# Attention scores computed in quarters of the TensorE array for the first 8 and the last 7 groups

## The chip, the cores and the metric

The kernel runs on one core of one Trainium2 chip. The metric is the device time of one execution in microseconds (us), lower is better. PE is TensorE (matmuls), PEld its weight loads, DVE is VectorE, ACT is ScalarE, POOL is GpSimd, SP is SyncE, whose queue issues the DMAs.

## What is computed

```python
def reference(q, k, v, w_gate, w_val, w_out, w_in2, w_out2):
    # q, k, v: 4 batches x 8 heads x 576 positions x 64
    scores = np.where((rel >= 0) & (rel < 64), q @ k.T / 8, -1e9)   # rel = row - column
    x = softmax(scores) @ v                    # as 2304 tokens x 512
    g = x @ w_gate                             # 512 x 1536
    x = (g * sigmoid(g) * (x @ w_val)) @ w_out # 1536 x 512
    h = x @ w_in2                              # 512 x 2048
    return (h * np.clip(h + 3, 0, 6) / 6) @ w_out2
```

Inputs and outputs are float32; the weights arrive as 64-bit floats.

## The kernel before

**Attention** is cut into 36 groups: 9 stretches of 256 tokens by 4 pairs of heads, numbered `n = stretch * 4 + pair`. A group goes through five parts, each a function: `scores` (PE), `softmax_a` and `softmax_b` (DVE and ACT), `transposes` (PE), `evac_t` (a copy out of PSUM), `values` (PE) and `store_x` (a copy into the tokens `xr`, or through a tile `xg` to memory). A group holds four blocks of 64 queries (`GB = 4`). In `scores` the two heads of a pair share one matmul of the whole 128x128 array: the queries of head 0 stand in rows 0 to 63 and columns 0 to 63 of the stationary operand, those of head 1 in the other two 64s, and the rest of it is zeros, written by the host. So one group loads 128 partitions of 512 numbers of queries and 320 of keys (832 x 128 float32, 416 KB), and its scores are four matmuls into one PSUM bank. A float32 matmul stands in the trace as two matmul instructions. `values` uses halves of the array: an output of 64 rows for each head.

**Main part.** The first feed-forward layer takes the tokens in blocks of 512 (`t` = 0, 1, 2) and chunks `c` of 128 of the 1536 columns: 36 steps `n = 12 t + c`. A step's own matmuls are `gate` (12, into PSUM bank `g`), `val` (12, into `v`) and `ffn1_out` of the step before (12, into four `acc` banks), in a form with operands split into a high and a low part. The first 8 groups run before step 0 (`first_block`). The other 28 are threaded through the steps: `group_at` says which group's scores stand at the end of which step; its softmax and transposes come one step later, its values two. Before, groups 8 to 15 have steps 1 to 8, groups 16 to 25 steps 11 to 20, and groups 26 to 35 steps 22 to 31. Scores go to bank `c` and transposes to bank `d` at the end of a step, behind `ffn1_out`, and values to `d` between `gate` and `val`. Meanwhile `pump` runs the conversion of the 64-bit weights (tiles `raw`, `wf`, `wt`, `ws`) on ACT and DVE a few operations at a time.

**Order.** `first_block` and everything from step 24 on are in program order on every engine; steps 1 to 23 are ordered by the framework's scheduler.

**Later parts.** The last 768 tokens go through the first layer by a scheme with fewer products (`wide_chunk`). Then comes a loop over chunks `c` (`late_out`, the late outputs): each step of it has 12 matmuls with a moving operand of 384 columns, whose operand `uh`/`ul` was split one step ahead by `late_split` (a copy on ACT, a subtraction on DVE). Beside it `prep` makes the operands of the second feed-forward layer (`operands`: `upper` on ACT, `lower` and `minus` on DVE) in 11 pieces, two per step. The rest of the time is the second layer.

Of the kernel before, what the change touches and what calls it, by code (L numbers as in the profile page):

```python
# [19 lines left out]
B, H, S, D = 4, 8, 576, 64  # L20
WIN = 64
# [8 lines left out]
TB = 512  # L30
# [22 lines left out]
CONVERT_STOP = 12  # L53
LATER = -5
LATER_FROM = 26
FIRST_LOADS = (3, 5)
CONVERT_WIDE = (0, 0, 0, 1, 1, 1, 2)
SUMS_WIDE = (3, 1, 1, 1, 0, 0, 0)
X_STEPS = {7: 1, 8: 1, 9: 1, 10: 1, 11: 1}
SAVE_FROM = 6  # L60


# [4 lines left out]
@with_exitstack  # L67
def attention_two_ffn(ctx: ExitStack, tc, qk, v, w, out):
    nc = tc.nc
# [274 lines left out]
    def masks():  # L344
        nc.gpsimd.memset(mask, 0.0)
        for h in range(2):
            a = mask[64 * h:64 * h + 64, 0, :]
            nc.gpsimd.affine_select(
                out=a, in_=a, compare_op=ALU.is_ge, fill=MASKED / SCALE,
                base=-1, pattern=[[1, 128]], channel_multiplier=-1,  # L350
            )
            nc.gpsimd.affine_select(
                out=a, in_=a, compare_op=ALU.is_ge, fill=MASKED / SCALE,
                base=WIN, pattern=[[-1, 128]], channel_multiplier=1,
            )
        nc.gpsimd.memset(mask[:, 1, 0:64], MASKED / SCALE)
        nc.vector.tensor_copy(mask[:, 1, 64:128], mask[:, 0, 64:128])
        make_identity(nc, ident)
# [9 lines left out]
    def load_qk(n):  # L368
        t = a_tile("qk", [128, GB * 128 + WIN + GT])
        nc.sync.dma_start(out=t, in_=qk[n])  # L370
        a_held[n, "qk"] = t
# [6 lines left out]
    def scores(n, tag):  # L378
# [8 lines left out]
        a_held[n, "s"] = s  # L387

    def softmax_a(n):
        s = a_held.pop((n, "s"))  # L390
        y = a_tile("y", [128, GB, 128])
        nm = a_tile("s", [128, 3, GB])
        for u in range(GB):
            m = 1 if (n // NPAIR * GB + u) % (S // WIN) == 0 else 0
            nc.vector.tensor_tensor_reduce(  # L395
                out=y[:, u, :], in0=s[:, u * 128:(u + 1) * 128], in1=mask[:, m, :],
                scale=-SCALE, scalar=3.0e38, op0=ALU.add, op1=ALU.min,
                accum_out=nm[:, 0, u:u + 1],
            )
# [27 lines left out]
    def evac_t(n):  # L427
        t = a_held.pop((n, "t"))
        pt = a_tile("pt", [128, GB, 128])
        on_act = n % 2 or per_block <= n < 2 * per_block  # L430
        copy = nc.scalar.copy if on_act else nc.vector.tensor_copy
        copy(pt.rearrange("p a b -> p (a b)"), t)
        a_held[n, "pt"] = pt

    def values(n, tag, bufs=1):
        pt = a_held.pop((n, "pt"))
        vt = a_held.pop((n, "v"))
        o = psum(tag, bufs)
        for u in range(GB):
            for h in range(2):  # L440
                rows = slice(h * D, (h + 1) * D)
                nc.tensor.matmul(
                    o[rows, u * WIN:(u + 1) * WIN], vt[:, u, rows],
                    pt[:, u, h * WIN:(h + 1) * WIN], start=True, stop=True,
                )
        a_held[n, "o"] = o

    def store_x(n, xr):
        g, p = n // NPAIR, n % NPAIR
        o = a_held.pop((n, "o"))  # L450
        copy = nc.scalar.copy if n < 2 * per_block or n % 2 else nc.vector.tensor_copy
        if n < n_wide:
# [23 lines left out]
    def first_block():  # L476

        xr = new_x()
        with ExitStack() as st:
# [8 lines left out]
            for s in range(per_block + 6):  # L488
# [7 lines left out]
                at(softmax_b, s - 2)  # L496
                at(scores, s, "gc"[s % 2])
                at(transposes, s - 3, "vd"[s % 2])
# [471 lines left out]
    steps1 = [(t, c) for t in range(NB) for c in range(NC1)]  # L970
    group_at = {n: per_block + n - 1 for n in range(1, per_block + 1)}
    group_at.update({n + LATER + (n >= LATER_FROM): n for n in range(2 * per_block, n_groups)})

# [4 lines left out]
    with ExitStack() as fixed:  # L978
# [10 lines left out]
        for n, (t, c) in enumerate(steps1):  # L989
            if n == 0:  # L990
                start.enter_context(tc.manual_schedule())
            if n == 1:
                start.close()
# [11 lines left out]
            gate(t, c, both=last)  # L1005
            at(softmax_a, n - 1)
            pump(pumps // 2)
            at(softmax_b, n - 1)
# [4 lines left out]
            u = silu(t, c)  # L1013
            at(values, n - 2, "d" if t else "c")
            at(load_v, n - 1)
            at(store_x, n - 2, xr)
            val(t, c)
# [5 lines left out]
            if n:  # L1023
                ffn1_out(*steps1[n - 1])
            at(transposes, n - 1, "d")
            at(scores, n, "c")
            at(evac_t, n - 1)
# [60 lines left out]
        for c in range(NC1 - 1):  # L1088
            load_ring()
            late_split(c + 1)  # L1090
            late_out(c)
            advance(prep, 2)
        for _ in prep:
# [25 lines left out]
def _layout(q, k, v, w_gate, w_val, w_out, w_in2, w_out2):  # L1119
# [3 lines left out]
    def by_head(a):  # L1123

        return a.reshape(B, NPAIR, 2, S, D).transpose(1, 2, 0, 3, 4).reshape(NPAIR, 2, NT, D)

    qd = np.zeros((NG, NPAIR, 2, D, GB, 2, WIN), q.dtype)
    qr = by_head(q).reshape(NPAIR, 2, NG, GB, WIN, D).transpose(1, 2, 0, 5, 3, 4)
# [4 lines left out]
    kt = np.stack([kp[..., g * GT:g * GT + GT + WIN] for g in range(NG)])  # L1133
    qk = np.concatenate([qd.reshape(n, 128, GB * 128), kt.reshape(n, 128, GT + WIN)], axis=2)
    vp = np.zeros((B, NPAIR, 2, WIN + S, D), v.dtype)
    vp[:, :, :, WIN:] = v.reshape(B, NPAIR, 2, S, D)
# [11 lines left out]
    w = np.concatenate([w1.reshape(-1, 128, 512), w2.reshape(-1, 128, 512)])  # L1148
    return {"qk_t": c(qk), "v_t": vt, "w_t": c(w).view(np.int64)}

# [22 lines left out]
```

## Time and profile before

| | us |
|---|---|
| median of 3 runs (931.14 to 934.33) | 932.47 |
| the profiled execution | 935.44 |
| its span on the core | 933.7 |
| PE busy / DVE busy / ACT busy in the span | 901.0 / 703.3 / 418.1 |

The span reaches from the first to the last instruction; the 1.7 us that the execution's time has more lie around it. Times in the rows further down are us from the start of the span. Ends of matmuls are modelled, so what a piece of PE work costs is best read from the start of one row to the start of the next.

### The profile page before, as it was taken

What the parts mean: (1) busy time and instruction counts of PE and PEld (TensorE: products, weight loads), DVE (VectorE), ACT (ScalarE), POOL (GpSimd) and SP (SyncE); (2) the same over time, 40 slices, a digit from 0 to 9 for tenths busy, and PEclk for the clock granted to TensorE, in tenths of its full rate; (3) what the DMA queues carried; (4) which work ended last, traced back from release to release, by engine and by line L of the source; (5) the groups of instructions that cost most, each with busy time, mean ns of one, the idle gap of its engine ahead of it and who ended that gap; (6) DMA issues with size and microseconds to landing.
All of it is one profiled execution on the core that took longest, in us unless ns stands there. A gap on an engine that the chain in (4) does not pass through costs nothing.

```text
span 933.7 us, 14252 instructions
## 1 busy us (share of the span) xinstructions
PE 901.0 (97%) x4968; PEld 790.2 (85%) x4968; DVE 703.3 (75%) x1628; ACT 418.1 (45%) x995; POOL 2.2 (0%) x12
## 2 busy tenths in 40 slices
PE   5699999998999999999999999999999999999997
PEld 5587787887777888789999899898989898989896
DVE  6999999987987887788888647766666677565654
ACT  5778897656765755534444423121122121311111
POOL 0000000000000000000000000000000000000000
PEclk9799999999999999999999999999999999999999
DMA  8557997777885888507454487856568656485601
GB/s 328 168 166 215 359 336 280 266 244 254 265 314 182 305 315 273 191 6 241 148 175 141 169 327 278 297 196 210 180 244 306 217 191 216 152 321 190 216 23 68
DMA packets 67607, 209.47 MB, mean 224 GB/s; under 512 B 7248, under 2 KB 14416, under 8 KB 67152
## 3 DMA queue, kind: packets, MB, share of 16 engines
q1 hardware_dynamic: 67392, 208.43, 64.5%
q8 instruction: 39, 0.64, 0.3%
q14 instruction: 32, 0.26, 0.1%
q10 hardware_dynamic: 144, 0.13, 0.0%
HBM read 159.12 MB, written 49.41 MB: 223 GB/s over the span
## 4 chain that ended last, share of the span: by engine, by line
PE 69%; DVE 12%; DMA 11%; ACT 5%; issue 2%; SPq 0%; ACTq 0%; DVEq 0%
DMA raw<-w_t 7%; PE acc L859 5%; PE acc L860 5%; PE acc L858 5%; PE v L817 3%; PE v L819 3%; PE v L818 3%; PE g L817 3%; PE g L819 3%; PE g L818 3%; PE acc L561 3%; PE acc L562 3%; PE acc L560 3%; DMA w2d<-ws 2%; PE v L510 2%
## 5 line engine op out<-in xcount | busy, mean ns | idle before, releaser
L838 ACT CAST gh<-g 128x384 fp32r<-128x384 f32 x96 | 49.3, 514 | 195.9 <-DVE g L829 171.2
L840 DVE TENSOR_TENSOR gl<-g,gh 128x384 fp32r<-128x384 f32 x96 | 53.2, 555 | 45.3 <-ACT gh L838 43.9
L561 PE MATMUL acc<-ul,wt 128*128 128x512 f32 (+1 forms) x216 | 81.6, 378 | 0.5 <-DVE ul L538 0.5
L562 PE MATMUL acc<-uh,wt 128*128 128x512 f32 (+1 forms) x216 | 80.3, 372 | 0.0
L860 PE MATMUL acc<-wt,gl 128*128 128x512 f32 x192 | 75.2, 391 | 0.0
L859 PE MATMUL acc<-wt,gh 128*128 128x512 f32 x192 | 75.1, 391 | 0.0
L858 PE MATMUL acc<-wt,gh 128*128 128x512 f32 x192 | 74.7, 389 | 0.0
L560 PE MATMUL acc<-uh,wt 128*128 128x512 f32 (+1 forms) x216 | 73.4, 373 | 0.9 <-ACT uh L533 0.7
L510 PE MATMUL g<-xh,wt 128*128 128x512 f32 x144 | 60.2, 418 | 6.5 <-DVE u L546 4.1
L132 ACT ACTIVATE raw<-raw 128x512 int32<-128x512 uint32 x68 | 46.1, 679 | 42.1 <-DMA raw<-w_t 41.6
L401 ACT ACTIVATE y<-y,s 128x128 f32<-128x128 f32 x144 | 56.2, 394 | 14.6 <-DVE s L395 14.4
L510 PE MATMUL v<-xh,wt 128*128 128x512 f32 x144 | 58.4, 406 | 0.0
L511 PE MATMUL g<-xl,wt 128*128 128x512 f32 x144 | 57.8, 401 | 0.2 <-DVE xl L330 0.2
L512 PE MATMUL g<-xh,wt 128*128 128x512 f32 x144 | 57.5, 399 | 0.0
L817 PE MATMUL v<-xh,wt 128*128 128x384 f32 x168 | 56.8, 338 | 0.4 <-ACT q L904 0.4
L817 PE MATMUL g<-xh,wt 128*128 128x384 f32 x168 | 56.5, 337 | 0.0
L511 PE MATMUL v<-xl,wt 128*128 128x512 f32 x144 | 56.5, 393 | 0.0
L512 PE MATMUL v<-xh,wt 128*128 128x512 f32 x144 | 56.5, 392 | 0.0
L819 PE MATMUL v<-xh,wt 128*128 128x384 f32 x168 | 56.4, 336 | 0.0
L819 PE MATMUL g<-xh,wt 128*128 128x384 f32 x168 | 56.4, 336 | 0.0
L818 PE MATMUL v<-xl,wt 128*128 128x384 f32 x168 | 56.3, 335 | 0.0
L818 PE MATMUL g<-xl,wt 128*128 128x384 f32 x168 | 56.3, 335 | 0.0
(202 smaller groups left out, 2276.0 us busy)
## 6 DMA issues: line engine op xcount, KB each, us to landing
wt<-w2d SPq DMA_DIRECT2D x144, 512.0 KB, 4.8
raw<-w_t SPq DMA_DIRECT2D x68, 512.0 KB, 5.0
w2d<-ws SPq DMA_DIRECT2D x48, 512.0 KB, 4.7
wt<-w1d SPq DMA_DIRECT2D x33, 512.0 KB, 4.3
qk<-qk_t SPq DMA_DIRECT2D x36, 416.0 KB, 5.2
w1d<-wt SPq DMA_DIRECT2D x26, 512.0 KB, 5.4
v<-v_t SPq DMA_DIRECT2D x36, 256.0 KB, 4.9
x_out<-ob SPq DMA_DIRECT2D x17, 256.0 KB, 2.1
```

The lines of the kernel that those rows point to most:

```text
L510: nc.tensor.matmul(dst, wt[:, 0, col], hi, start=kc == 0, stop=False)
L511: nc.tensor.matmul(dst, wt[:, 0, col], lo, start=False, stop=False)
L512: nc.tensor.matmul(dst, wt[:, 1, col], hi, start=False, stop=kc == KC - 1)
L560: nc.tensor.matmul(a, wt[:, 0, col], hi, start=c == 0, stop=False)
L561: nc.tensor.matmul(a, wt[:, 0, col], lo, start=False, stop=False)
L562: nc.tensor.matmul(a, wt[:, 1, col], hi, start=False, stop=c == NC1 - 1)
L817: nc.tensor.matmul(dst, wt[:, 0, col], hi[:, k, :], start=k == 0, stop=False)
L818: nc.tensor.matmul(dst, wt[:, 0, col], lo[:, k, :], start=False, stop=False)
L819: nc.tensor.matmul(dst, wt[:, 1, col], hi[:, k, :], start=False, stop=k == 1)
L858: nc.tensor.matmul(a, hi[:, row], wt[:, 0, :], start=begin, stop=False)
L859: nc.tensor.matmul(a, hi[:, row], wt[:, 1, :], start=False, stop=False)
L860: nc.tensor.matmul(a, lo[:, row], wt[:, 0, :], start=False, stop=end)
```

## The change

Three things are done. **First**, groups 0 to 7 and 29 to 35 (`QUARTERS`) get their scores by `quarter_scores`: for each block of queries and each head one matmul with a stationary operand of 64 x 64 (no zeros) and 128 moving columns. The head sets the half of the array's rows, the parity of the block the half of its columns, so that four matmuls that follow each other lie in four quarters; head 0 writes to one PSUM bank and head 1 to another. Such a group loads 576 x 128 float32 (288 KB), from an input of its own. Softmax and values take the blocks in the new order; softmax has the same number of operations. **Second**, the groups stand at other steps: 8 to 15 at steps 1 to 8, group 24 at step 10, 16 to 23 at steps 11 to 18, 25 to 35 at steps 19, 20 and 22 to 30. From step 24 on, transposes (now in bank `v`), values (in the second half of bank `c`) and quarter scores (in the first halves of `c` and `d`) stand one behind the other at the end of the step, and `store_x` moves to the start of the next step but one; for groups 29 and up `evac_t` is always on ACT and `store_x` on DVE. **Third**, the loop of the late outputs makes one piece of `prep` per step in place of two. Around this, a part of the mask that belongs to the first block of a sequence is first written by GpSimd in two halves, since blocks now share a softmax operation's rows differently, and filled up at step 0.

```diff
-LATER = -5
-LATER_FROM = 26
...
+LAST_FROM, LAST_STEP = 29, 24
+EMPTY = (9, 21)
+QUARTERS = [*range(TB // GT * (H // 2)), *range(LAST_FROM, NG * (H // 2))]
+WHOLE = [n for n in range(NG * (H // 2)) if n not in QUARTERS]
...
-        nc.gpsimd.memset(mask[:, 1, 0:64], MASKED / SCALE)
+        nc.gpsimd.memset(mask[0:64, 1, 0:64], MASKED / SCALE)
+        nc.gpsimd.tensor_copy(mask[64:128, 1, 0:64], mask[64:128, 0, 0:64])
...
     def load_qk(n):
-        t = a_tile("qk", [128, GB * 128 + WIN + GT])
-        nc.sync.dma_start(out=t, in_=qk[n])
+        if n in QUARTERS:
+            t = a_tile("qk", [128, GT + WIN + GT])
+            nc.sync.dma_start(out=t, in_=qq[QUARTERS.index(n)])
+        else:
+            t = a_tile("qk", [128, GB * 128 + WIN + GT])
+            nc.sync.dma_start(out=t, in_=qk[WHOLE.index(n)])
...
+    def quarter_scores(n, s):
+
+        t = a_held.pop((n, "qk"))
+        for u in range(GB):
+            for h in range(2):
+                rows = slice(h * D, (h + 1) * D)
+                k0 = GT + u * WIN
+                nc.tensor.matmul(
+                    s[h][u % 2 * WIN:(u % 2 + 1) * WIN, u // 2 * 128:(u // 2 + 1) * 128],
+                    t[rows, u * WIN:(u + 1) * WIN], t[rows, k0:k0 + 128],
+                    start=True, stop=True,
+                )
+        a_held[n, "s"] = s
...
-        on_act = n % 2 or per_block <= n < 2 * per_block
+        on_act = n % 2 or per_block <= n < 2 * per_block or n >= LAST_FROM
...
-        copy = nc.scalar.copy if n < 2 * per_block or n % 2 else nc.vector.tensor_copy
+        on_act = n < 2 * per_block or n % 2 and n < LAST_FROM
+        copy = nc.scalar.copy if on_act else nc.vector.tensor_copy
...
-                at(scores, s, "gc"[s % 2])
+                if s < per_block:
+                    quarter_scores(s, [psum("acc", 4) for _ in "ab"] if s % 2 else [psum("g"), psum("c")])
...
-    group_at = {n: per_block + n - 1 for n in range(1, per_block + 1)}
-    group_at.update({n + LATER + (n >= LATER_FROM): n for n in range(2 * per_block, n_groups)})
+    order = [*range(8, 16), 24, *range(16, 24), *range(25, n_groups)]
+    group_at = dict(zip((n for n in range(1, 36) if n not in EMPTY), order))
...
+                nc.gpsimd.memset(mask[64:128, 1, 0:64], MASKED / SCALE)
...
             at(softmax_a, n - 1)
+            if n >= LAST_STEP:
+                at(store_x, n - 3, xr)
...
-            at(values, n - 2, "d" if t else "c")
-            at(load_v, n - 1)
-            at(store_x, n - 2, xr)
+            if n < LAST_STEP:
+                at(values, n - 2, "d" if t else "c")
+                at(load_v, n - 1)
+                at(store_x, n - 2, xr)
...
-            at(transposes, n - 1, "d")
-            at(scores, n, "c")
+            if n < LAST_STEP:
+                at(transposes, n - 1, "d")
+                at(scores, n, "c")
+            elif n in group_at or n - 2 in group_at:
+                both = psum("c"), psum("d")
+                at(transposes, n - 1, "v")
+                at(values, n - 2, both[0][:, GT:])
+                at(quarter_scores, n, both)
+                at(load_v, n - 1)
...
-            advance(prep, 2)
+            advance(prep, 1)
```

The order of the instructions on PE in a late step, before: the end of `ffn1_out` (bank `acc`), transposes (L424), scores (L383) and the next step's `gate` (bank `g`).

```order
L562 MATMUL acc<-uh,wt 128x512
L424 MATMUL d<-ident,y 128x128 x4
L383 MATMUL c<-qk 128x128 x4
L510 MATMUL g<-xh,wt 128x512
L511 MATMUL g<-xl,wt 128x512
```

Further on in the same step, before, the values (L442) stand between the end of `gate` and the start of `val` (bank `v`).

```order
L512 MATMUL g<-xh,wt 128x512
L442 MATMUL d<-pt,v 64x64 x8
L510 MATMUL v<-xh,wt 128x512
L511 MATMUL v<-xl,wt 128x512
```

The same late step in the change: transposes (L452), values (L471) and the eight quarter scores (L403), between the end of `ffn1_out` (L593) and the next `gate` (L541).

```order
L593 MATMUL acc<-uh,wt 128x512
L452 MATMUL v<-ident,y 128x128 x4
L471 MATMUL c<-pt,v 64x64 x8
L403 MATMUL c<-qk 64x128
L403 MATMUL d<-qk 64x128
L403 MATMUL c<-qk 64x128
L403 MATMUL d<-qk 64x128
L403 MATMUL c<-qk 64x128
L403 MATMUL d<-qk 64x128
L403 MATMUL c<-qk 64x128
L403 MATMUL d<-qk 64x128
L541 MATMUL g<-xh,wt 128x512
```

So the values have left the place between `gate` and `val`, and everything that attention has on PE in such a step stands in one place, in the order transposes, values, scores.

At step 24, where program order begins, PE has before, in the midst of the step, transposes of one group directly ahead of that group's values (which read the copy that `evac_t` makes of the transposes).

```order
L512 MATMUL g<-xh,wt 128x512
L424 MATMUL d<-ident,y 128x128 x4
L442 MATMUL d<-pt,v 64x64 x8
L510 MATMUL v<-xh,wt 128x512
L511 MATMUL v<-xl,wt 128x512
```

In the change that pair stands at the end of the step, with the transposes of the next group between.

```order
L593 MATMUL acc<-uh,wt 128x512
L452 MATMUL d<-ident,y 128x128 x4
L452 MATMUL v<-ident,y 128x128 x4
L471 MATMUL c<-pt,v 64x64 x8
L403 MATMUL c<-qk 64x128
```

What moved is the wait of the values for the copy: four transposes lie in it now, and `evac_t` of that group is on ACT, where it was on DVE.

DVE beside the late outputs, before: the subtraction for the next chunk (L538), `lower` (L769) and `minus` (L775) of the second layer's operands.

```order
L538 TENSOR_TENSOR ul<-us,uh 128x384
L769 TENSOR_TENSOR xl<-xb,xh 128x768
L775 TENSOR_TENSOR xb<-xb 128x768
L538 TENSOR_TENSOR ul<-us,uh 128x384
L769 TENSOR_TENSOR xl<-xb,xh 128x768 x2
L538 TENSOR_TENSOR ul<-us,uh 128x384
L775 TENSOR_TENSOR xb<-xb 128x768 x2
L538 TENSOR_TENSOR ul<-us,uh 128x384
```

And in the change (the lines are L569, L800 and L806 there):

```order
L569 TENSOR_TENSOR ul<-us,uh 128x384
L800 TENSOR_TENSOR xl<-xb,xh 128x768
L569 TENSOR_TENSOR ul<-us,uh 128x384
L806 TENSOR_TENSOR xb<-xb 128x768
L569 TENSOR_TENSOR ul<-us,uh 128x384
L800 TENSOR_TENSOR xl<-xb,xh 128x768
L569 TENSOR_TENSOR ul<-us,uh 128x384
L800 TENSOR_TENSOR xl<-xb,xh 128x768
```

Each operation for the second layer now has a subtraction for the late outputs on either side, all 11 chunks long.

## Rows read from the trace of the kernel before

**Rows 1.** The page's part 1: busy us, share of the span and instructions of each engine.

```profile
PE 901.0 (97%) x4968; PEld 790.2 (85%) x4968; DVE 703.3 (75%) x1628; ACT 418.1 (45%) x995; POOL 2.2 (0%) x12
```

**Rows 2.** Busy time by stage: stretch, length, engines, granted clock, DMA share, GB/s.

```profile
0.00:41.20 41.20, 24.24 (x224) 20.95 (x224) 30.91 (x119) 28.32 (x96) 2.25 (x12) 0.87 0.74 259
41.20:288.50 247.30, 241.48 (x1372) 195.26 (x1372) 221.90 (x579) 181.26 (x454) 0.00 (x0) 0.99 0.76 261
288.50:409.40 120.90, 118.41 (x702) 97.07 (x699) 94.68 (x234) 68.42 (x178) 0.00 (x0) 1.00 0.69 238
526.10:552.40 26.30, 24.74 (x133) 22.70 (x133) 16.38 (x24) 10.76 (x19) 0.00 (x0) 1.00 0.94 363
```

**Rows 3.** Timeline of PE, first block: start, us, operation, [idle before, what ended it].

```profile
4.21 2.08 PE L383 MATMUL g<-qk 128*128 128x128 f32 x8 [4.21 <-DMA qk<-qk_t]
...
20.14 1.72 PE L383 MATMUL c<-qk 128*128 128x128 f32 x8 [4.13 <-DMA qk<-qk_t]
21.65 1.06 PE L424 MATMUL d<-ident,y 128*128 128x128 f32 x4
...
41.26 0.80 PE L510 MATMUL g<-xh,wt 128*128 128x512 f32 x1 [2.37 <-ACT xh L329]
```

**Rows 4.** Timeline of DVE, first block.

```profile
22.75 0.69 DVE L432 COPY pt<-d 128x512 f32<-128x512 f32 x1 [2.43 <-PE d L424]
```

**Rows 5.** DMA traffic from 2.4 to 20.4 us.

```profile
DMA packets 2174, 6.38 MB, mean 354 GB/s; under 512 B 239, under 2 KB 239, under 8 KB 2173
```

**Rows 6.** Timeline of PE, a late step with attention, its successor's start, and a step without attention.

```profile
331.27 0.60 PE L424 MATMUL d<-ident,y 128*128 128x128 f32 x4
331.70 1.06 PE L383 MATMUL c<-qk 128*128 128x128 f32 x8
332.51 0.47 PE L510 MATMUL g<-xh,wt 128*128 128x512 f32 x1
...
335.43 0.69 PE L442 MATMUL d<-pt,v 128*64 128x64 f32 x16
336.05 0.50 PE L510 MATMUL v<-xh,wt 128*128 128x512 f32 x1
...
341.63 0.60 PE L424 MATMUL d<-ident,y 128*128 128x128 f32 x4
...
393.16 0.39 PE L510 MATMUL g<-xh,wt 128*128 128x512 f32 x1
...
401.32 0.39 PE L510 MATMUL g<-xh,wt 128*128 128x512 f32 x1
```

**Rows 7.** Weight loads of values by line: busy, mean ns of one, idle before.

```profile
L442 PEld LDWEIGHTS d<-pt,v 128*64 128x64 f32 x320 | 11.0, 137 | 8.9 <-DVE u L546 2.1 <-ACT raw L132 1.1 <-DVE s L410 1.1
```

**Rows 8.** Waits of PE from 288.5 to 409.4: total us, times, longest.

```profile
PE d L442 <- DVE u L546: 1.9, 1, 1.9
PE d L442 <- DMA v<-v_t: 0.6, 1, 0.6
```

**Rows 9.** Longest wait of PE in total from 41.2 to 288.5.

```profile
PE g L510 <- DVE u L546: 4.1, 5, 1.9
```

**Rows 10.** Timeline of PE, late outputs: first matmul of chunks 0, 2, 4, 7; second layer.

```profile
526.10 0.33 PE L560 MATMUL c<-uh,wt 128*128 128x384 f32 x1
...
530.87 0.45 PE L560 MATMUL c<-uh,wt 128*128 128x384 f32 x1 [0.44 <-ACT uh L533]
...
536.54 0.44 PE L560 MATMUL c<-uh,wt 128*128 128x384 f32 x1 [0.68 <-ACT uh L533]
...
544.13 0.33 PE L560 MATMUL c<-uh,wt 128*128 128x384 f32 x1
...
552.45 0.33 PE L817 MATMUL g<-xh,wt 128*128 128x384 f32 x1
```

**Rows 11.** Timeline of ACT, late outputs, ahead of chunk 4.

```profile
534.51 1.57 ACT L763 CAST xh<-xb 128x768 fp32r<-128x768 f32 x2 [3.29 <-DVE xb L775]
```

**Rows 12.** Instructions on tile `xb`: count, ns min/median/max, first and last start.

```profile
L769 DVE TENSOR_TENSOR xl<-xb,xh x21: 948/951/958, 527.6 to 789.8; 128x768 fp32r<-128x768 f32 x21
```

More of the change, by code (lines that the diff above doesn't have):

```diff
@@ L67, in attention_two_ffn @@
 @with_exitstack
-def attention_two_ffn(ctx: ExitStack, tc, qk, v, w, out):
+def attention_two_ffn(ctx: ExitStack, tc, qk, qq, v, w, out):
     nc = tc.nc
@@ L393, in softmax_a @@
         for u in range(GB):
-            m = 1 if (n // NPAIR * GB + u) % (S // WIN) == 0 else 0
+            if n in QUARTERS:
+                f = n // NPAIR * GB + u % 2 * 2
+                assert (f + 1) % (S // WIN)
+                m = 1 if f % (S // WIN) == 0 else 0
+                su = s[u // 2][:, u % 2 * 128:(u % 2 + 1) * 128]
+            else:
+                m = 1 if (n // NPAIR * GB + u) % (S // WIN) == 0 else 0
+                su = s[:, u * 128:(u + 1) * 128]
             nc.vector.tensor_tensor_reduce(
-                out=y[:, u, :], in0=s[:, u * 128:(u + 1) * 128], in1=mask[:, m, :],
+                out=y[:, u, :], in0=su, in1=mask[:, m, :],
                 scale=-SCALE, scalar=3.0e38, op0=ALU.add, op1=ALU.min,
@@ L437, in values @@
         vt = a_held.pop((n, "v"))
-        o = psum(tag, bufs)
+        o = psum(tag, bufs) if isinstance(tag, str) else tag
         for u in range(GB):
@@ L441, in values @@
                 rows = slice(h * D, (h + 1) * D)
+                a, b = (2 * h + u // 2, u % 2) if n in QUARTERS else (u, h)
                 nc.tensor.matmul(
                     o[rows, u * WIN:(u + 1) * WIN], vt[:, u, rows],
-                    pt[:, u, h * WIN:(h + 1) * WIN], start=True, stop=True,
+                    pt[:, a, b * WIN:(b + 1) * WIN], start=True, stop=True,
                 )
@@ L1125, in by_head @@
         return a.reshape(B, NPAIR, 2, S, D).transpose(1, 2, 0, 3, 4).reshape(NPAIR, 2, NT, D)
+    qq = by_head(q).reshape(NPAIR, 2, NG, GT, D).transpose(2, 0, 1, 4, 3)
     qd = np.zeros((NG, NPAIR, 2, D, GB, 2, WIN), q.dtype)
@@ L1134, in _layout @@
     qk = np.concatenate([qd.reshape(n, 128, GB * 128), kt.reshape(n, 128, GT + WIN)], axis=2)
+    qq = np.concatenate([qq.reshape(n, 128, GT), kt.reshape(n, 128, GT + WIN)], axis=2)
     vp = np.zeros((B, NPAIR, 2, WIN + S, D), v.dtype)
@@ L1148, in _layout @@
     w = np.concatenate([w1.reshape(-1, 128, 512), w2.reshape(-1, 128, 512)])
[L1149 removed]
+    return {"qk_t": c(qk[WHOLE]), "qq_t": c(qq[QUARTERS]), "v_t": vt, "w_t": c(w).view(np.int64)}
 def kernel(**inputs):
```

## The prediction

> **What bounds the kernel now.** I began with busy times: PE is busy 97% of the span [rows 1], so a change counts only where PE gets less work or where PE waits. The table by stage then shows where it waits [rows 2]. In the first 41.2 us PE is busy 24.2 us, DVE 30.9, and the DMA engines are 74% busy: PE does not bound that stage. From 41.2 to 288.5 PE is busy 241.5 of 247.3 us, with DVE close behind (221.9). From 288.5 to 409.4 PE has 118.4 of 120.9 us and DVE 94.7: PE alone is the bound. The late outputs, 526.1 to 552.4, have 24.7 of 26.3, and the start-to-start times will show that they lose more than this.
>
> In the first block the timelines show one hard stop: the sixth group's scores wait 4.13 us for their queries and keys [rows 3], and because PE takes its queue in order, the transposes behind them wait too, until DVE itself sits idle 2.43 us for those transposes [rows 4]. Up to there the DMA engines moved 354 GB/s without a pause [rows 5].
>
> In a late step everything fits together without a gap [rows 6]. From one step's transposes to the next step's (331.27 to 341.63) it is 10.36 us; a step without attention takes 8.16 (393.16 to 401.32). Attention costs PE 2.20 us in such a step: transposes 0.43, scores 0.81, values 0.62 (each from its start to the next row's), and the remaining 0.34 is what the step's own matmuls lose around them.
>
> **The change, term by term**, against the profiled execution of 935.4 us.
>
> *First block.* A group's load shrinks from 832 to 576 numbers per partition, 416 to 288 KB. Up to the sixth group that is 6 x 128 KB = 0.79 MB, 2.2 us at 354 GB/s [rows 5]. Its scores took 1.51 us (20.14 to 21.65), the first group's 2.08 [rows 3]; in quarters perhaps half of that. So the transposes for which DVE waits could come some 3 us earlier, but DVE can win only its own idle time, 2.43 us [rows 4], and the little by which the first groups run ahead. I take 2.4. Lower bound 1.0, if what DVE then waits for is the next load in the same queue; upper 3.4, if the earlier start of the first groups (half of 2.08) carries through as well. Whatever is won is kept if the first `gate`, at 41.26 [rows 3], moves with it: it waits for the copies at the end of DVE's and ACT's work, not for a fixed time.
>
> *Scores in quarters, in one place.* Four transposes take 0.43 us, 0.108 for 128 columns [rows 6]. The 16 instructions of the values have 64 columns each, so one after another they would take 16 x 0.054 = 0.86 us; they take 0.62, so the two halves of the array do work side by side (8 x 0.054 = 0.43, and 0.19 for the turn to other work). The 16 instructions of the quarter scores have 128 columns: 1.72 us one after another, 0.86 two at a time, 0.43 four at a time. No row shows two halves of the rows side by side. The nearest row is the values', whose halves of the columns do overlap, and I take four at a time. The place then holds transposes 0.43, values 0.43, scores 0.43, and turns: 0.19 behind the last of them, and about 0.2 for the lead-in of `gate`, whose 12 matmuls from 332.51 to 335.43 take 2.92 where a third of a bare step is 2.72. Together 1.7 in place of 2.20, 0.5 in each of 7 steps (24 to 30): 3.5 us. With no turn but one it is 1.5 (4.9 us won), with three full turns 1.9 (2.1 won).
>
> The Trainium skill has a rule that speaks against this: TensorEngine Tiling (Array Packing), under Key Properties, says that a change of the tiling mode, not merely of the tile, drains TensorE. The 0.19 behind the values agrees with it. By that rule the place has three such turns (whole array, halves, quarters, whole array) at 0.19, which makes 1.86 us and 2.4 us won in place of 3.5; the forecast below would be 1.1 us higher.
>
> *Waits from 288.5 to 409.4.* PE has two there, both ahead of values: 1.9 us at step 24, where the values stand right behind their own group's transposes and must wait for the copy, and 0.6 for a load [rows 8]. In the change the first has four more transposes (0.43) in between and its copy on ACT; the second's values stand several us later in the step. What is late next is the same copy; I leave 0.6 us for it and for transposes that must wait until `val`'s result has been read from bank `v`. Won: 1.9 of 2.5 (bounds 0.5 and 2.5).
>
> *Group 24 at step 10.* Eight groups had their scores from step 24 on, now seven have. Its 2.20 us of PE leave the last stage and enter the one before it: nothing in the sum. But there DVE is busy 90% of the time against 78% later [rows 2], and the scheduler places anew everything from step 10 to 23. Bounds from PE's longest waits there, 4.1 us in five places [rows 9]: 3 better, 5 worse. I take 1.1 worse, half of the group's 2.20, as if PE and DVE shared the price.
>
> *Late outputs.* From 544.13 to 552.45 four chunks run without a wait: 2.08 each. Eleven make 22.9, but the loop takes 26.35 [rows 10]: 3.45 us are lost, in the first chunks only, where PE waits for `uh`. ACT was held up by two copies for the second layer, which themselves waited 3.29 us for DVE's `minus` [rows 11]. With one piece per step DVE has 0.95 us [rows 12] and a subtraction to do in 2.08 us, and ACT at most one such copy (0.8) and one `uh`. I take 3.4 won. The lower bound is 0: the memory of the first layer's tokens comes free up to five steps later, and the weights that follow into it cross DMA engines that are 94% busy [rows 2]. The first four of those weights, for the second layer's first unit, come into places that PE frees, so I expect no wait.
>
> *At no price*: the mask writes on GpSimd (busy 2.2 us in all [rows 1]), and copies that change between ACT and DVE, under PE's 118 us [rows 2]; uncovered, each would cost the difference of two copies, about 0.1 us.
>
> Sum: -2.4 - 3.5 - 1.9 + 1.1 - 3.4 = -10.1, so 925.3 us beside the profiled 935.4. The median of the runs, 932.5, is 2.9 lower than that execution, so I predict **922.4 us**.
>
> **Rivals.**
> 1. *Two at a time, or no better.* If the halves of the rows take turns, or every turn is dear, the quarter group costs 0.86, the place 2.13, and 0.5 us is left of 3.5: 925.4. For it: no row shows halves of the rows together. Against it: the two heads write to different banks.
> 2. *The middle gets worse.* Steps 10 to 23 in a new order with one group more, where DVE and the weight loads are nearly full. Three more waits like the longest one, 1.9 us [rows 9], in place of my 1.1: about 927, with a spread from 924 to 935.
> 3. *The late outputs win nothing*, because the second layer waits for what the loop no longer loses: 925.8. Against it: those weights have a whole unit's time to come in.
> 4. *The other side: quarter loads in line.* If the weight load of each quarter (137 ns for 64 columns [rows 7]) is not hidden behind another quarter's matmul, a group costs 16 x (0.137 + 0.108) = 3.9 us, 3.5 more than I count, in 7 steps with PE as the bound: 922.4 + 24 = 947. It decides for slower from about 2.3 us a group, (10.1 + 2.8) / 7 above 0.43. Against it: the values' loads of that length are hidden, 16 of them in 0.62 us.
>
> **How the numbers follow.** About 0.3%, 2.8 us, is what a measurement of this kernel can tell from no change: faster is below 929.7, slower above 935.3. Chances: the forecast 0.50, rival 1 0.18, rival 2 0.20, rival 3 0.08, rival 4 0.04. Faster are the forecast and rivals 1 and 3 (0.76) and 0.05 of rival 2; within 0.3% is 0.11 of rival 2; slower 0.04 of it and rival 4. That is 0.81, 0.11 and 0.08. The likeliest case alone reaches from 918 (the upper bounds, 3.4 + 4.9 + 2.5 + 3.45, with the middle unchanged) to 926. The range goes down to 917 and up to 930, across rivals 1 and 3 and the better part of rival 2.
>
> **What would show each step.** The sixth group's scores start at about 18 us and the first `gate` at about 38.8. In a late step the quarter scores take about 0.45 us from their first start to the next `gate`, plus a turn, and the step about 9.9 us in place of 10.36. The 1.9 us wait at step 24 is down to half a us. The late outputs take 23 us, with `uh` never waited for. The second layer's length stays as it is. The forecast is wrong if the stage from step 1 to 23 is more than 4 us longer than its 247.3, if the quarter scores take 0.9 us or more, or if waits for weights appear at the start of the second layer.

## The result and the profile after

The changed kernel takes 920.98 us (median of 4 runs, 919.49 to 922.33) beside 931.81 for the kernel before on the same chip: a ratio of 0.988, 95% interval 0.985 to 0.991, so 8.3 to 13.8 us less. (A fourth run of the kernel before took its median from 932.47 to 931.81.) The forecast was 922.4 (917 to 930). The total is right; three of its five terms are not, as the stages show.

Part 1 of the page after (busy us, share of the span, instructions of each engine):

```profile
PE 893.4 (97%) x5088; PEld 781.3 (85%) x5088; DVE 701.9 (76%) x1629; ACT 417.8 (45%) x994; POOL 2.7 (0%) x14
```

PE has 7.6 us less to do and is as full as before [rows 1]. The windows by stage after: stretch, length, PE, PEld, DVE, ACT, POOL busy, granted clock, DMA share, GB/s. They answer to [rows 2]: first block, steps 0 to 23, step 24 to the wide part, late outputs.

```profile
0.00:39.45 39.45, 21.86 (x289) 16.40 (x289) 30.64 (x120) 28.23 (x96) 2.68 (x14) 0.79 0.74 252
39.45:283.00 243.55, 241.53 (x1383) 194.90 (x1384) 221.93 (x586) 183.39 (x465) 0.00 (x0) 0.99 0.78 267
283.00:400.45 117.45, 115.41 (x743) 93.00 (x742) 93.15 (x228) 65.83 (x164) 0.00 (x0) 1.00 0.66 231
517.10:540.00 22.90, 22.90 (x134) 22.90 (x134) 16.35 (x24) 11.08 (x19) 0.00 (x0) 1.00 0.93 357
```

From this pair of profiles the first block is 1.8 us shorter, steps 0 to 23 3.7, the stage from step 24 on 3.4, the late outputs 3.5 and the second layer 1.2 (381.2 to 380.0). Only the first block and the late outputs stand where the forecast put them; the second layer was to keep its length.

PE's timeline after, first block (the sixth group's scores, the first `gate`), to be laid beside [rows 3]:

```profile
18.63 1.23 PE L403 MATMUL acc<-qk 64*64 64x128 f32 x16 [4.13 <-DMA qk<-qq_t]
...
39.45 0.80 PE L541 MATMUL g<-xh,wt 128*128 128x512 f32 x1 [2.37 <-ACT xh L331]
```

The scores stand 1.5 us earlier and wait as long as before: everything ahead of the load has moved with it.

PE's timeline after, the place at the end of step 28, a step without a wait: transposes, values, the sixteen instructions of the quarter scores, the next `gate`. It answers to [rows 6].

```profile
334.76 0.60 PE L452 MATMUL v<-ident,y 128*128 128x128 f32 x4
335.29 0.69 PE L471 MATMUL c<-pt,v 128*64 128x64 f32 x16
335.90 0.32 PE L403 MATMUL c<-qk 64*64 64x128 f32 x1
335.91 0.32 PE L403 MATMUL d<-qk 64*64 64x128 f32 x1
335.92 0.32 PE L403 MATMUL c<-qk 64*64 64x128 f32 x1
335.92 0.32 PE L403 MATMUL d<-qk 64*64 64x128 f32 x1
336.06 0.27 PE L403 MATMUL c<-qk 64*64 64x128 f32 x1
...
336.30 0.27 PE L403 MATMUL d<-qk 64*64 64x128 f32 x1
336.50 0.50 PE L541 MATMUL g<-xh,wt 128*128 128x512 f32 x1
```

Four quarter instructions start within 0.02 us of each other, so four do run at a time: first start to last start is 0.40 us. Then come 0.20 to `gate`. The place takes 1.74 us from 334.76 to 336.50, and `gate` 0.13 more than a third of a bare step (2.85 against 2.72): 1.87. The step is 10.04 long, against 10.36.

PE's waits after, from step 24 to the wide part (total us, times, longest):

```profile
PE c L471 <- DMA v<-v_t: 1.1, 1, 1.1
PE v L452 <- DVE u L584: 0.8, 2, 0.6
```

Neither is in [rows 8]: the values wait for their own load, and the transposes wait until `times_val` (L584) has read bank `v`. Steps 24 to 30 take 12.47, 10.16, 10.36, 10.44, 10.04, 10.84 and 10.08 us (start of `gate` to start of `gate`). Against 10.04, steps 25 to 29 lose 1.6, in front of the transposes.

The late outputs after, first matmul of the loop and of the second layer; between them PE has no wait, where the loop of [rows 10] lost 3.45 us:

```profile
517.11 0.33 PE L591 MATMUL c<-uh,wt 128*128 128x384 f32 x1
...
539.99 0.33 PE L848 MATMUL g<-xh,wt 128*128 128x384 f32 x1
```

### The profile page after: what moved, and what is told of

It is laid out like the page before. It is cut to its first block, busy times and chain, and to the rows that moved or that the text cites. A ratio compares the mean times of both kernels' runs of the same rounds, so it can differ in the third digit from the quotient of the medians.

```text
span 920.0 us, 14498 instructions
## 1 busy us (share of the span) xinstructions
PE 893.4 (97%) x5088; PEld 781.3 (85%) x5088; DVE 701.9 (76%) x1629; ACT 417.8 (45%) x994; POOL 2.7 (0%) x14
## 4 chain that ended last, share of the span: by engine, by line
PE 69%; DMA 12%; DVE 10%; ACT 6%; issue 2%; SPq 0%; ACTq 0%; DVEq 0%
DMA raw<-w_t 8%; PE acc L890 5%; PE acc L891 5%; PE acc L889 5%; PE v L848 3%; PE v L850 3%; PE v L849 3%; PE g L848 3%; PE g L850 3%; PE g L849 3%; PE acc L592 3%; PE acc L591 3%; PE acc L593 3%; DMA w2d<-ws 2%; DVE wf L186 2%
## 5 line engine op out<-in xcount | busy, mean ns | idle before, releaser
L593 PE MATMUL acc<-uh,wt 128*128 128x512 f32 (+1 forms) x216 | 80.4, 372 | 0.0
L541 PE MATMUL g<-xh,wt 128*128 128x512 f32 x144 | 59.9, 416 | 3.6 <-ACT xh L331 2.4
L429 ACT ACTIVATE y<-y,s 128x128 f32<-128x128 f32 x144 | 56.3, 394 | 11.0 <-DVE s L423 10.8
L541 PE MATMUL v<-xh,wt 128*128 128x512 f32 x144 | 57.3, 398 | 0.0
```

The lines of the kernel that those rows point to most:

```text
L541: nc.tensor.matmul(dst, wt[:, 0, col], hi, start=kc == 0, stop=False)
L593: nc.tensor.matmul(a, wt[:, 1, col], hi, start=False, stop=c == NC1 - 1)
```

## Experiments

One table for all: stages in us, from the starts of `gate` in each profile. A profile is one execution, so kernels that share a stage's program show how far executions differ.

| kernel | first `gate` | step 0 | steps 1 to 23 | step 24 to wide part | late loop |
|---|---|---|---|---|---|
| before | 41.26 | 9.08 | 238.25 | 120.89 | 26.35 |
| 1 one operand a step | 42.02 | 8.58 | 236.34 | 119.58 | 22.88 |
| 2 first 8 in quarters | 37.60 | 8.14 | 236.76 | 119.11 | 26.31 |
| 3 groups' order | 42.30 | 8.24 | 239.26 | 122.53 | 26.31 |
| the change | 39.45 | 7.86 | 235.72 | 117.46 | 22.88 |
| 4 padded loads | 39.64 | 8.33 | 239.99 | 119.02 | 22.88 |
| 5 whole scores last | 39.65 | 7.91 | 235.61 | 120.21 | 22.88 |
| 6 scores twice | 39.92 | 9.06 | 233.46 | 119.07 | 22.88 |
| 7 in two parts | 37.63 | 8.30 | 235.44 | 118.68 | 22.88 |
| 8 transposes last | 39.90 | 8.85 | 235.21 | 116.77 | 22.88 |
| 9 `times_val` first | 39.39 | 8.67 | 237.39 | 116.71 | 22.88 |
| 10 both mends | 39.32 | 8.32 | 234.19 | 117.53 | 22.88 |
| 11 and a second `v` | 40.02 | 8.93 | 234.10 | 116.92 | 22.88 |
| 12 less conversion | 37.80 | 9.04 | 235.82 | 114.99 | 22.95 |

Before, 1 and 2 have the same order of matmuls in steps 1 to 23; so have 3, 5 to 12 and the change; 4 has an order of its own.

### 1. One operand a step, alone

```diff
 # in the kernel before
-            advance(prep, 2)
+            advance(prep, 1)
```

> The kernel before with one piece of the second layer's operands beside each late output, and nothing else of the change. My theory (the late outputs lose 3.45 us to operands that DVE and ACT make too early): the loop takes 22.9 us where it took 26.35, never waits for uh or ul, and the second layer keeps its length, so the kernel gains 3.4 us: about 928.4 beside 931.8. Rival (the second layer waits for what the loop no longer loses): the loop is shorter, the second layer's first units longer by as much, and the time stays at 931.8. Up to the late outputs this kernel is the one before, so its stages there also show how far two executions of one program differ.

928.1 us (8 runs) beside 932.2; ratio 0.9956 (0.9938 to 0.9974). The loop's first matmul and the second layer's, in this kernel's timeline:

```profile
523.13 0.33 PE L560 MATMUL c<-uh,wt 128*128 128x384 f32 x1
...
546.01 0.33 PE L817 MATMUL g<-xh,wt 128*128 128x384 f32 x1
```

22.88 us, no wait for `uh` or `ul`, and the second layer not longer (380.0 us, 381.2 before). The theory holds; rival 3 of the forecast is out. The same program up to here as before, it also shows the looseness of one profile: the first `gate` 0.8 later, steps 1 to 23 1.9 shorter, and the wait at step 24 [rows 8] is 0.8 where it was 1.9:

```profile
PE d L442 <- DVE pt L432: 0.8, 1, 0.8
```

Experiment 2, which has other loads in the first block but the same late steps, has 0.8 there too.

### 2. Quarter scores for the first 8 groups alone

```diff
 # in the changed kernel
-LAST_FROM, LAST_STEP = 29, 24
+LAST_FROM, LAST_STEP = 99, 99
-QUARTERS = [*range(TB // GT * (H // 2)), *range(LAST_FROM, NG * (H // 2))]
+QUARTERS = [*range(TB // GT * (H // 2))]
 # groups' steps and advance(prep, 2) as before
```

> Quarter scores and their smaller loads for the first 8 groups alone, with the mask that goes with them; groups, late steps and late outputs as before. My theory: the first block ends 1.8 us earlier, as in the changed kernel (first gate at 39.45 where it was 41.26), and the gate and val of step 0 take 7.9 us in place of 9.1, because the stretch at half clock reaches 1.3 us less far into them; 3.0 us in all, 928.8. Rival 1 (the stretch at half clock lies where chance puts it): step 0 takes 9 us or some third value and the gain is 1.8 alone, 930. Rival 2 (the middle is ordered anew because it starts from another state, and gives the time back): steps 1 to 23 take over 240 us and nothing is left.

926.8 us (6 runs) beside 932.2; ratio 0.9938 (0.9916 to 0.9960), 3.7 to 7.8 us less. The first `gate` stands at 37.60. Step 0 at 8.14 leaves the half-clock theory where rival 1 had it: over all kernels with the small loads step 0 takes 7.9 to 9.1, as it does before (8.2 to 9.1), and the granted clock in it is 0.64 before, 0.72 here, 0.75 in the change and 0.64 again in experiment 6. So the first block's end is what is won, with 2.8 us between the means of three kernels (41.9) and ten (39.1). The gain in time is larger than that mean; why is open, beyond the spread of the first `gate`, 37.6 to 40.0.

### 3. The groups' order alone

```diff
 # in the kernel before
-    group_at = {n: per_block + n - 1 for n in range(1, per_block + 1)}
-    group_at.update({n + LATER + (n >= LATER_FROM): n for n in range(2 * per_block, n_groups)})
+    order = [*range(8, 16), 24, *range(16, 24), *range(25, n_groups)]
+    group_at = dict(zip((n for n in range(1, 36) if n not in (9, 21)), order))
```

> The kernel before with the change's table of groups alone (group 24 at step 10, 16 to 23 one step earlier or in place, 25 to 35 at 19, 20 and 22 to 30). My first theory, after the changed kernel's trace: steps 1 to 23 are shorter there (235.7 us against 238.3) although they hold a group more, because the scheduler's new order takes away the waits of 4.1 us. Then this kernel's steps 1 to 23 take 235 to 237 us, the stage from step 24 on loses one group's 2.2 us (118.7 in place of 120.9), and the kernel gains 4 to 5 us: 927 to 928. Rival 1 (the forecast's own term: the middle gets dearer by the group that it takes): steps 1 to 23 take 240 us or more, the last stage 118.7, and the time stays within 1.5 us of 931.8. Rival 2 (the gain comes from loads and an earlier start that the quarter scores allow): steps 1 to 23 as before plus a group, 240.5 us, the same time.

931.7 us (12 runs) beside 932.2; ratio 0.9992 (0.9973 to 1.0011). My first theory is refuted as far as the time goes. Rival 1 has the time right and its stages wrong: 239.3 and 122.5 us, not 240 or more and 118.7. The profiled execution (937.1) shows a place that can give the gain back. PE's timeline at step 24, where old-style values, transposes and values again share bank `d`:

```profile
292.75 0.69 PE L442 MATMUL d<-pt,v 128*64 128x64 f32 x16
295.55 0.65 PE L424 MATMUL d<-ident,y 128*128 128x128 f32 x4 [2.11 <-DVE xg L462]
296.88 1.12 PE L442 MATMUL d<-pt,v 128*64 128x64 f32 x16 [0.68 <-ACT pt L432]
```

And the windows of that stretch and of `val` behind it:

```profile
292.75:297.93 5.18, 2.39 (x37) 1.90 (x37) 4.63 (x10) 2.20 (x5) 0.00 (x0) 0.84 0.60 220
297.93:303.15 5.22, 5.22 (x14) 4.13 (x13) 0.00 (x0) 0.89 (x2) 0.00 (x0) 0.51 0.61 177
```

Step 24 takes 17.3 us there, against 12.85 or less. How much of that the other 11 runs have, their times don't say. Their granted clocks say a little: the 12 runs have 0.9876 on average, 19 of the kernel before 0.9903. One stretch of 5.2 us at 0.51 would make 0.0027 of it (an estimate: 5.2 x 0.49 of 935 us), so as much time at the lower clock is likely in most of them; where it lies is not shown.

### 4. Padded loads in the first block

```diff
 # in the changed kernel
-            t = a_tile("qk", [128, GT + WIN + GT])
-            nc.sync.dma_start(out=t, in_=qq[QUARTERS.index(n)])
+            wide = GB * 128 + WIN + GT if n < per_block else GT + WIN + GT   # the host pads qq
+            t = a_tile("qk", [128, wide])
+            nc.sync.dma_start(out=t, in_=qq[QUARTERS.index(n)][:, :wide])
```

> The changed kernel with the loads of the first 8 groups padded back to 416 KB (832 numbers per partition, of which 576 are used). My theory: bytes set the start of the sixth group's scores; six groups of 128 KB more at 354 GB/s are 2.2 us, the scores start at 20.2 or later and the first gate at about 41.2 where the three kernels with the small loads have it at 37.6, 39.45 and 39.9; the time is 922.5 to 923.5. Rival: PE's shorter scores (1.2 us for the sixth group in place of 1.5, 0.9 in place of 2.1 for the first) did it, the first gate stays at 39 and the time at 921.

```profile
18.81 1.02 PE L404 MATMUL acc<-qk 64*64 64x128 f32 x12 [3.46 <-DMA qk<-qq_t]
...
39.64 0.79 PE L542 MATMUL g<-xh,wt 128*128 128x512 f32 x1 [2.38 <-ACT xh L331]
```

With the old bytes the sixth group's scores start at 18.81 and the first `gate` stands at 39.64, in the midst of the kernels with small loads (37.6 to 40.0, mean 39.1). My theory falls: the 2.2 us of bytes are not needed. What the shorter scores do shows in SP's waits up to 16 us, before and here. A load of queries and keys is issued when scores have freed a tile `qk`, and SP waits 2.1 and 1.9 us for that before, twice 1.2 here, as in the change:

```profile
SPq L370 <- PE g L383: 2.1, 1, 2.1
SPq L370 <- PE c L383: 1.9, 1, 1.9
```

```profile
SPq L375 <- PE acc L404: 1.2, 1, 1.2
SPq L375 <- PE c L404: 1.2, 1, 1.2
```

The sixth group's load is issued at 12.07 before, at 11.25 here and at 10.22 in the change. The scores of the first block also write to other banks than before; that was not tested by itself.

The time, 927.0 (ratio 0.9944, 0.9927 to 0.9961), is no answer to this: the scheduler ordered steps 1 to 23 anew beside the longer loads, and they take 4.3 us more than in the change. In this profile PE waits 2.1 us there ahead of 220.3 and 1.9 ahead of 255.7, and the granted clock is 0.71 from 220 to 225 and 0.66 from 255 to 260. The late steps, which are those of the change, take 119.0 us in place of 117.5, with 2.6 us of waits for bank `v`. The late outputs and the second layer take what they take in the change.

### 5. Whole scores for the last 7 groups, in the one place

```diff
 # in the changed kernel: QUARTERS for the first 8 only, and
-                at(quarter_scores, n, both)
+                at(scores, n, both[1])      # scores() takes a bank too
```

> The changed kernel with whole-array scores again for the last seven groups (into bank d, and with their larger loads), all in the one place at the end of a step. My theory: the quarters themselves are what shortens a late step. In the changed kernel the place costs 1.87 us of a step (transposes 0.53, values 0.62, quarter scores 0.40 and a turn of 0.2, lead-in of gate 0.13), and steps without a wait take 10.04 to 10.08; with whole scores (0.81) they take 10.36 again, as before. Seven steps: 2.2 us more than the changed kernel less what the wait for bank v gives back (up to 1), 922 to 923.2. Rival: the one place is what saves, by one turn less, and the quarters nothing; then steps without a wait take 10.05 and the time is 921.

923.5 us beside 932.8; ratio 0.9901 (0.9885 to 0.9917). The place in a step without a wait:

```profile
314.32 0.60 PE L452 MATMUL v<-ident,y 128*128 128x128 f32 x4
314.85 0.69 PE L471 MATMUL c<-pt,v 128*64 128x64 f32 x16
315.46 1.16 PE L390 MATMUL d<-qk 128*128 128x128 f32 x8
316.38 0.48 PE L541 MATMUL g<-xh,wt 128*128 128x512 f32 x1
```

The scores take 0.91 to `gate`, quarters 0.60: such a step is 10.35 long. The quarters save 0.31 us a step, 2.2 in seven. But the stage is 2.75 longer than the change's: the wait for bank `v` grew to 2.4 us in four steps instead of shrinking. So in this profile the one place by itself is dearer than the old late steps, which had no such wait: 120.2 against 117.7 (the mean of three, 119.9, less the group of 2.2 that left). The time is not told apart from the change's.

### 6. Scores twice

```diff
 # in the changed kernel
+                if n in group_at:
+                    twice = a_held[group_at[n], "qk"]
+                    quarter_scores(group_at[n], both)
+                    a_held[group_at[n], "qk"] = twice
                 at(quarter_scores, n, both)
```

> The changed kernel with the 8 quarter scores of each of the last seven groups issued twice (the same result written a second time), which prices them without a turn. My theory, four at a time: 0.43 us a step more, steps without a wait 10.47 and 3.0 us in all, 924. Rival 1, two at a time: 0.86 a step, 6.0 in all, 927. Rival 2, the weight loads in line: 3.9 a step, 27 in all, 948.

925.1 us beside 932.8; ratio 0.9922 (0.9903 to 0.9941). Steps without a wait take 10.47 to 10.54, 0.43 to 0.50 more than 10.04. Four at a time. Rival 4 of the forecast is out, and of rival 1 the two at a time; its other half, dear turns, is experiment 7.

### 7. Values and scores in two parts that alternate

```diff
 # in the changed kernel; values and quarter_scores take the blocks in `part`
-                at(values, n - 2, both[0][:, GT:])
-                at(quarter_scores, n, both)
+                for part in ((0, 1), (2, 3)):
+                    at(values, n - 2, both[0][:, GT:], 1, part)
+                    at(quarter_scores, n, both, part)
```

> The changed kernel with values and quarter scores of a late step each cut into two parts that alternate (values of blocks 0 and 1, scores of blocks 0 and 1, values of 2 and 3, scores of 2 and 3): the same matmuls, two changes between halves and quarters more. My theory, which is now the drain that the forecast weighed: each change costs 0.15 to 0.2 us, a step 0.3 to 0.4 more, steps without a wait 10.4, and the kernel 2.1 to 2.8 more, 923.5. Rival: what I took for a turn is the lead-in of gate and of transposes alone, and changes between halves and quarters cost nothing; steps without a wait stay at 10.05 and the time at 921.

```profile
312.52 0.60 PE L452 MATMUL v<-ident,y 128*128 128x128 f32 x4
313.05 0.45 PE L472 MATMUL c<-pt,v 128*64 128x64 f32 x8
313.44 0.32 PE L403 MATMUL c<-qk 64*64 64x128 f32 x1
...
313.81 0.45 PE L472 MATMUL c<-pt,v 128*64 128x64 f32 x8
314.20 0.32 PE L403 MATMUL c<-qk 64*64 64x128 f32 x1
...
314.57 0.50 PE L542 MATMUL g<-xh,wt 128*128 128x512 f32 x1
```

The same matmuls take 2.05 us where they took 1.74: 0.31 for two changes more between halves and quarters, 0.15 each, and 10.36 us for a step without a wait. The theory holds in the place. In the time, where 923.5 was expected, it does not show: 920.7 beside 932.8 (0.9876, 0.9855 to 0.9896), not told apart from the change; the 1.2 us of the stage are within what runs differ by.

### 8 to 11. Mending the new waits

```diff
 # 8, in the changed kernel
-                at(transposes, n - 1, "v")
                 at(values, n - 2, both[0][:, GT:])
                 at(quarter_scores, n, both)
+                at(transposes, n - 1, "v")
 # 9, in the changed kernel
             val(t, c)
-            pump(pumps)
+            if n < LAST_STEP:
+                pump(pumps)
             times_val(t, c, u)
+            if n >= LAST_STEP:
+                pump(pumps)
 # 10: both. 11: both, and "v": 2 in place of "v": 1 in open_attention
```

> The changed kernel with the place at the end of a late step in the order values, quarter scores, transposes (it was transposes, values, quarter scores). My theory (in the changed kernel steps 26, 27 and 29 are 0.3 to 0.8 us too long because the transposes wait until times_val has read bank v): the transposes stand 1.2 us later, that wait is gone, steps 25 to 30 take 10.0 to 10.1 us each (60.4 in all where they took 61.9), and the values of step 24, which wait for their load, wait 0.5 us longer; 1.0 us less than the changed kernel, about 920. Rival 1 (what is late is DVE and ACT altogether, and the wait moves to the next reader): some other wait of the same size, val for the copy out of bank v above all, and steps 25 to 30 take 61.5 or more. Rival 2 (a turn costs more in this order): no wait, but every step takes 10.3 or more.

> The changed kernel with times_val ahead of the conversion's operations on DVE from step 24 on (it stood behind them), and nothing else. My theory: the transposes' wait for bank v is made by DVE's queue, where times_val stands behind two or three conversion operations of 0.6 us each after a late silu; then the waits at L452 are gone, steps 25 to 30 take 60.3 to 60.6 us in all where they took 61.9, and the kernel gains 1.5: 919.5. Rival 1: silu itself is late (its tanh stands behind the softmax's work on ACT), and the wait only shrinks: 61.2 or more. Rival 2: what was pushed behind is late next (ul, or the loads of raw), and waits of PE for ul or for weights take its place: 61.9 again.

> The changed kernel with both mends: the order values, quarter scores, transposes in the place, and times_val ahead of the conversion's operations from step 24 on. My theory: each of steps 25 to 30 takes 9.99 us, 60.0 in all, 1.9 less than in the changed kernel, and the time is about 919, at the edge of what can be measured. Rival: as for the two mends alone, a wait for another reader comes up, and steps 25 to 30 take 61 or more.

> Both mends and a second buffer for the values' operand v from step 1 on, so that the load for step 24 can start before the values ahead of it have been computed. My theory: the values of step 24 wait no more for their load (1.0 to 1.1 us), step 24 takes 11.4 in place of 12.4, and the time is about 918. Rival: loads that start earlier stand ahead of the weights in the same queue, and the middle, whose order of loads changes, gives it back: steps 1 to 23 take 237 or more and the time is 919 to 920.

What the mends were after, in the change at step 29: DVE's timeline, `times_val` (L584) behind a late `silu` (L577) and three operations of the conversion, and PE's transposes behind it.

```profile
342.20 0.69 DVE L577 SCALAR_TENSOR_TENSOR u<-u,g 128x512 f32<-128x512 f32 x1 [1.66 <-ACT u L576]
342.81 0.69 DVE L186 SCALAR_TENSOR_TENSOR wf<-raw,wf 128x512 uint32<-128x512 uint32 x1
343.53 0.69 DVE L192 CUSTOM_DVE_ANT_0 wf<-raw,wf 128x1024 uint16<-128x1024 uint16 x1
344.14 0.68 DVE L199 TENSOR_TENSOR ws<-wf,ws 128x512 fp32r<-128x512 f32 x1
344.74 0.68 DVE L584 TENSOR_TENSOR u<-v,u 128x512 f32<-128x512 f32 x1
```

```profile
345.57 0.63 PE L452 MATMUL v<-ident,y 128*128 128x128 f32 x4 [0.60 <-DVE u L584]
```

Measured: 920.8 (ratio 0.9875, 0.9848 to 0.9903), 922.9 (0.9901, 0.9887 to 0.9916), 921.3 (0.9894, 0.9876 to 0.9912) and 922.4 us (0.9901, 0.9885 to 0.9918). Steps 25 to 30 take 61.4, 62.0, 61.8 and 61.9 us where the change has 61.9. Mend 8 wins a third of what was expected, the others nothing. In 8 no new reader comes up: the transposes, 1.2 us later, still wait for `times_val` in steps 28 and 29. PE's waits from step 24 on in 8:

```profile
PE c L471 <- DMA v<-v_t: 1.0, 1, 1.0
PE v L452 <- DVE u L584: 1.0, 2, 0.8
```

In 9 that wait shrinks to 0.2 and in 10 and 11 it is gone, but others take its place, as the rival of 10 had it and, at other readers than it named, the second rival of 9. The longest waits in 9, in 10 and in 11:

```profile
PE c L471 <- DMA v<-v_t: 0.5, 1, 0.5
PE v L541 <- ACT pt L460: 0.4, 1, 0.4
```

```profile
PE c L471 <- DMA v<-v_t: 2.3, 2, 1.4
```

```profile
PE c L471 <- DMA v<-v_t: 1.3, 1, 1.3
PE c L471 <- ACT pt L460: 0.7, 1, 0.7
```

In 9 to 11 the wait goes to whichever is late next: a load of `v`, the copy out of bank `v`. In 11 the second buffer ends the wait for the load at step 24, as expected, but 0.7 us for the copy stands there then, and step 28 waits 1.3 for its load. None of these kernels is told apart from the change as faster.

### 12. Less conversion beside the late steps

```diff
 # in the changed kernel
-CONVERT = (8, 5, 5)
+CONVERT = (8, 5, 2)
```

> The changed kernel with 6 operations of the weight conversion in each step from step 24 on where it has 15; what is left undone is done later, beside the wide part and ahead of the late outputs, so the whole time says little and is expected to be longer (930 to 945, since DVE has only some 17 us to spare in the wide part). What counts is the stage from step 24 to the wide part. My theory, after the mends moved the waits without shortening them: what holds up PE in the late steps is the conversion that shares ACT, DVE and the DMA queue with attention, and which reader of a bank or of a load waits for it is an accident of the order. Then steps 25 to 30 take 10.04 to 10.1 each, 60.4 in all in place of 61.9, with no wait at L452 or L471, and step 24 takes 11.2 to 11.6. Rival: the waits are made by attention's own chain (scores, softmax, transposes, copy, one step each), and the steps stay at 61.5 or more with the same waits.

PE's waits from step 24 to the wide part in this kernel, the whole list:

```profile
PE c L471 <- ACT pt L460: 0.2, 1, 0.2
```

And that stage's window:

```profile
282.70:397.60 114.90, 114.66 (x742) 93.18 (x741) 73.62 (x191) 55.03 (x143) 0.00 (x0) 1.00 0.50 172
```

Steps 25 to 30 take 60.30 us, 10.05 each; DVE is busy 64% of the stage where it was 79%. The theory holds: the conversion's share of ACT, DVE and the queue of loads makes the waits, and attention's own chain alone leaves 0.2 us, at step 24. Which of the three it is, this run doesn't tell. The time, 932.9 beside 933.8 (ratio 0.9995, 0.9983 to 1.0007), is as long as expected: from the start of step 35 to the late outputs, where the rest of the conversion now stands, it is 138.5 us in place of 124.8.

## Why the prediction was right, and where it was wrong

**Late outputs, -3.4.** Right in mechanism and size: 3.47, with this part alone and inside the change.

**First block, -2.4.** Right in size: 1.8 between the two profiles, 2.8 between means. The step "2.2 us at 354 GB/s" is not what carries it: padded loads leave the first `gate` at 39.64. What is won is the shorter scores' time on PE, which I had taken as the smaller part: SP waits 0.9 and 0.7 us less for the tiles of the next loads (experiment 4), so the loads themselves start earlier.

**Quarter scores in one place, -3.5.** The mechanism, four at a time, is right (0.40 from first to last start, 0.43 for a second set). The term was mis-sized: the place takes 1.87, not 1.7, and a step wins 0.32, not 0.5, so 2.2. The step that failed is "turns: 0.19 behind the last of them": there is one behind every part. In the place, the transposes take 0.53 to the values where whole scores follow them in 0.43 [rows 6], so their turn is 0.10; the values' 0.61 and the quarters' 0.60 hold nearly 0.2 each. The Trainium skill has the rule (TensorEngine Tiling (Array Packing), Key Properties) that a change of tiling mode drains TensorE. The trace agrees with it, at 0.1 to 0.2 us a change; that the forecast's sum by that rule, 1.86, comes so near 1.87 is in part luck, since it left out the 0.13 of `gate` and took the first turn at 0.19.

**Waits from 288.5 to 409.4, -1.9.** Wrong. The 1.9 us at step 24 was one execution's; experiment 1, the same program up to there, and experiment 2, with the same late steps, have 0.8. And the transposes in bank `v`, to which I gave 0.6 us together with the copy, cost 1.6 in steps 25 to 29, with 1.1 more for a load at step 24. Of the 5.4 us that these two terms promised, the late steps kept about 0.2 (119.9, less 2.2, against 117.5), and nothing in experiment 4's execution of the same late steps (119.0).

**Group 24 at step 10, +1.1.** Wrong in sign, by the means. The group's 2.2 us and the 1.1 should have made steps 1 to 23 longer; they take 233.5 to 239.3 us, mean 235.6 of ten kernels, where three with the old order take 236.3 to 238.3, mean 237.1. The middle had waits enough (4.1, 2.5 and 3.2 us for `u` alone in the three) to take the group in. That the new order made them fewer is seen, not shown, since ten executions of it differ by more than the two means, and the one with nothing but the order (experiment 3) has the 239.3.

Added up, from means where there are several: 2.8 for the first block, 0.1 in step 0, 1.5 for the middle, 2.4 for the stage from step 24 (the change's one profile; 0.9 by experiment 4's) and 3.5 for the late outputs make 10.3; the medians are 10.8 apart. The second layer, 381.2 us in the profiles of the kernel before and of experiment 2 and 379.9 to 380.2 in all others, is a term that the forecast had at nothing; experiment 3, with the old pieces of `prep`, has 379.9, so they don't explain it, and the cause stays open. The forecast had 10.1. It came out right by luck, because its errors cancelled: the stage from step 24 on was to win 7.6 with the group that leaves it and won 2.4, the middle was to lose 3.3 and won 1.5.

## What to carry to other kernels

A stage in which PE is 98% busy has little of its own to lose, but a helper that shares DVE, ACT and the load queue sets where PE waits: moving the reader that is late finds the same wait again or the next one, and taking helper work out is the test that tells. Before a term is hung on one wait in one profile, look at a second execution of the same steps: here the wait was 1.9 us in one and 0.8 in two. Small tiles pay by fours, less a turn for every change of the tiling, so like goes beside like.

## What the runs showed of the hardware

Matmuls of 64x64 by 128 columns in four quarters start 7 ns apart, and the fours follow each other after 0.16 and then 0.11 us; no weight load shows between them. A change between halves and quarters costs 0.15 us (experiment 7). The weight loads show where such a turn sits. Within one tiling a load runs ahead: in step 28 of the change that of the transposes starts at 334.53, 0.23 us before its matmul. At each of the three changes in that place the next load starts only with its own matmul. At the values PEld stands idle 0.17 us before it, at `gate` (336.50) again 0.17, at the quarters 0.07:

```profile
335.29 0.55 PEld L471 LDWEIGHTS c<-pt,v 128*64 128x64 f32 x16 [0.17 <-issue]
```

In the profiled execution of experiment 3, PE was busy 2.39 of 5.18 us at step 24, and in the 5.2 us behind it the granted clock was 0.51, near the lower level of 1.2 GHz: `val` took 5.22 us where it takes 2.7: behind waits of 2.1 and 0.7 us another 2.5 were lost. Experiment 4 has two such places, but a single wait of 1.9 us at step 24 of the kernel before [rows 8] is followed by no fall: the granted clock of that stage is 1.00 [rows 2].
